# Evacuating PV results with four masked VectorE operations and one row-sum product, in a decode kernel bound by its loads

## Chip, cores, metric

One core of one Trainium2 chip. The metric is the device time of one execution in microseconds (us); medians of several runs. The kernel before had 366.29 us (three runs, 366.27 to 366.82).

## The reference

A gated mix of two branches for 8 sequences of one token, `D` = 576:

```python
a = attention(x, k_cache, v_cache, wq, wo)   # 32 query heads on 16 KV heads, head size 128,
                                             # last 2048 positions of each cache
b = mlp(layernorm(x), w1, b1, w2, b2)        # 576 -> 4608 -> 576, gelu
out = g * a + (1 - g) * b                    # g = sigmoid(sum(x * gate_w))
```

The K and V windows are 67 MB each, the weights 20 MB; each byte is used once.

## The kernel before

Operations are handed to a list scheduler, which fixes each engine's order when the program is built. At run time an engine takes its list in order: what stands behind an operation that waits doesn't run before it. Loads stream in one queue: `wq, w1`, 16 K tiles of 4 MB with 32 V units of 2 MB between them, `wo`, the last V units, then the four W2 chunks. A unit is one KV head for four sequences. PV is the product of the softmax's probabilities P with V; its evacuation is the step that takes the result out of PSUM (`ps`), where TensorE writes, into SBUF. For a pair of units the tail of the attention looks so:

```python
# TensorE: PV of one unit; p.V leaves 4 diagonal blocks (r) that still have to be added over rows
for t in range(16):
    mm = e.matmul(ps[c:c + 32, bk, :], PT[...], slot(s)[:, 512 * t:512 * t + 512], ...)
...
# after the second unit of the pair: all 512 columns to SBUF by ScalarE
u_ev[item] = add("act", lambda e: e.activation(out=EV[:, item % 2, :], in_=ps[:, bk, :]..., func=ACTF.Copy), ...)
# four fp32 products, one for each diagonal block
for r in range(4):
    mm = e.matmul(ps[:, BK_S, ...], EV[:, item % 2, 128 * r:128 * r + 128], i2[:, r, :, :]..., start=(r == 0), stop=(r == 3))
# then: small copy (ScalarE), product with 1/sum (GpSimd; VectorE for the last pair), and
def place(ch, bs, deps):      # sixteen tiny VectorE copies that put the heads where the projection wants them
    return [add("dve", ... e.tensor_copy(oT[32*q:32*q+32, ch, j, bs], oN[32*j:32*j+32, q, ch, bs]) ...)
            for j in range(4) for q in range(4)]

def project():                # four output projections; the c-th waits for the c-th set of copies
    for c in range(4):
        ...
        AccGroup("proj%d" % c, mms, place_done[c] + ds, cost=1.1)
# W2 products, as each chunk lands, accumulate in the same bank; then the final sum on VectorE
o_m2.append(AccGroup("m2_%d_%d" % (ci, n), mms, [o_hT, d], ...).op)
```

Of the kernel before, what the change touches and what calls it, by code (L numbers as in the profile page):

```python
# [7 lines left out]
F32 = mybir.dt.float32  # L8
ACTF = mybir.ActivationFunctionType
ALU = mybir.AluOpType  # L10
AXL = mybir.AxisListType
# [27 lines left out]
class _Plan:  # L39
# [10 lines left out]
    def add(self, eng, fn, deps=(), name=None, cost=0.1, after=(), prio=0):  # L50
        op = _Op(eng, fn, deps, name, cost, after=after, prio=prio)
        op.idx = len(self.all)
        self.all.append(op)
        return op
# [116 lines left out]
ARENA_BASE = 16512  # L171


def held_matmul(nc, e, out, lhsT, rhs, start=False, stop=True, skip=False, tile_size=(128, 128), tile_position=(0, 0)):
    return e.add_instruction(mybir.InstMatmult(
        name=nc.get_next_instruction_name(), engine=mybir.EngineType.PE,
        ins=[e.lower_ap(rhs), e.lower_ap(lhsT)], outs=[e.lower_ap(out)],
        start_tensor_calc=start, stop_tensor_calc=stop, is_transpose=False, bass_skip_group_check=skip,
        tile_size=tile_size, tile_position=tile_position, ldweights=False))


def build_kernel(nc, A_x, A_k_cache, A_v_cache, A_wq, A_wo, B_x, B_w1, B_b1, B_w2, B_b2, gate_w, out):
    B, Sq, D = A_x.shape
    _, Hkv, Sk, Dh = A_k_cache.shape
# [22 lines left out]
    with ExitStack() as es:  # L207
# [3 lines left out]
        def req(name, nelem, dt, align=64):  # L211
            sz = 2 if dt == BF else 4
            o = aoff[0] + ARENA_BASE
            o = (o + align - 1) // align * align - ARENA_BASE
            R[name] = (o, nelem, dt)
            aoff[0] = o + nelem * sz
# [17 lines left out]
        req("q4", 4 * 256, BF)  # L234
        req("qb", 2 * 8 * 4 * 32, BF)
        req("amask", 4, F32)
        req("b1T", FT, F32)
        req("b2", D, BF)
        req("hT", FT * 8, BF)
# [36 lines left out]
        def aoffs(name):  # L276
            return R[name][0] // 2
# [4 lines left out]
        def view(name, parts=128):  # L282
            o, n, dt = R[name]
            a = arena[0:parts, o // 2: o // 2 + (n * (2 if dt == BF else 4)) // 2]
            if dt == F32:
                a = a.bitcast(F32)
            return a
# [6 lines left out]
        i2 = view("i2").rearrange("p (r u m) -> p r u m", r=4, u=2)  # L294
# [6 lines left out]
        q4 = view("q4").rearrange("p (h m) -> p h m", h=4)  # L301
        qb = view("qb").rearrange("p (g n h m) -> p g n h m", g=2, n=8, h=4)
        amask = view("amask")
        b1T = view("b1T")
        b2_sb = view("b2", 8)
        u_sb, uh_sb, v1_sb, v2_sb = view("u"), view("uh"), view("v1"), view("v2")
# [15 lines left out]
        EV = view("EV").rearrange("p (u n) -> p u n", u=2)  # L322
# [7 lines left out]
        def slot(s):  # L330
            return RAW[:, s * SE:(s + 1) * SE]
# [12 lines left out]
        ps = es.enter_context(nc.psum_tensor("ps", [128, 8, 512], F32))  # L344
# [4 lines left out]
        BK_S = 6  # L349
        BK_ACC = 7  # L350
        OC = 64
# [6 lines left out]
        add, dma = P.add, P.dma  # L358
# [38 lines left out]
        for s in range(2):  # L397
            o_xz.append(add("dve", (lambda s=s: lambda e: e.tensor_copy(xz[:, s, :].rearrange("p (k z) -> p k z", z=2)[:, :, s], x_sb[:, 512:576]))(),  # L398
                            deps=dx + [o_xz0], name="xz%d" % s, cost=0.12))
# [12 lines left out]
        for s in range(2):  # L412
            o_yz.append(add("dve", (lambda s=s: lambda e: e.tensor_copy(yz[:, s, :].rearrange("p (k z) -> p k z", z=2)[:, :, s], y_bf[:, 512:576]))(),
                            deps=[o_y, o_yz0], name="yz%d" % s, cost=0.12))
# [30 lines left out]
        def b1ev_fn(e):  # L445
# [5 lines left out]
                   deps=[o_dga, o_dgb, o_onesf], name="g_pe", cost=0.4, after=[o_yTp])  # L451
# [7 lines left out]
        o_i20 = add("dve", lambda e: e.memset(view("i2"), 0.0), name="i2z", cost=0.1, prio=-1)  # L459
        o_i2 = [add("dve", (lambda q=q: lambda e: e.tensor_copy(i2[32 * q:32 * q + 32, :, q // 2, :], ident[32 * q:32 * q + 32, 32 * q:32 * q + 32].rearrange("p (r m) -> p r m", r=4)))(),  # L460
                    deps=[o_i20, o_ident], name="i2_%d" % q, cost=0.15, prio=-1) for q in range(4)]
        for q in range(4):
            o_i32.append(add("dve", (lambda q=q: lambda e: e.tensor_copy(i32[32 * q:32 * q + 32, :], ident[32 * q:32 * q + 32, 32 * q:32 * q + 32]))(),
                             deps=[o_ident, o_obl], name="i32_%d" % q, cost=0.15, prio=-1))
# [67 lines left out]
        o_hT = add("dve", hs_fn, deps=[o_hf, o_gb], name="hT", cost=0.4)  # L532
# [50 lines left out]
        u_ev, u_sum = {}, {}  # L583
        b6_w, b6_r = [], [o_yT, o_gb]
# [116 lines left out]
        def v_compute(i, s, d):  # L701
            g, q = divmod(i, 4)
            item = 2 * g + q // 2

            bk = BK_OS[item % 2]

            def pv_fn(e):
                mm = None
                for t in range(16):
                    c = 64 * (i % 2) + 32 * (t % 2)  # L710
                    mm = e.matmul(ps[c:c + 32, bk, :], PT[:, g % 2, 512 * q + 32 * t:512 * q + 32 * t + 32], slot(s)[:, 512 * t:512 * t + 512],  # L711
                                  start=(t < 2), stop=(t >= 14), skip_group_check=True, tile_position=(0, c))
                return mm
            deps = [d] + pt_done[g] + ([u_ev[item - 2]] if item >= 2 else o_qT + [o_u])
            prev = add("pe", pv_fn, deps=deps, name="pv%d" % i, cost=1.9, after=pv_hist[-1:])
            pv_hist.append(prev)
            slot_free[s] = [prev]
            if q == 3:
                pv_last[g] = prev
            if i % 2 == 0:  # L720
                return
            u_ev[item] = add("act", lambda e: e.activation(out=EV[:, item % 2, :], in_=ps[:, bk, :].rearrange("p (r d j) -> p r j d", r=4, j=4), func=ACTF.Copy),  # L722
                             deps=pv_hist[-2:] + ([u_sum[item - 2]] if item >= 2 else [o_hT]), name="uev%d" % item, cost=1.2, prio=3)

            def us_fn(e):
                mm = None
                for r in range(4):
                    mm = e.matmul(ps[:, BK_S, OC + 16 * (item % 2):OC + 16 * (item % 2) + 16], EV[:, item % 2, 128 * r:128 * r + 128], i2[:, r, :, :].rearrange("p u m -> p (u m)"),  # L728
                                  start=(r == 0), stop=(r == 3), skip_group_check=True)
                return mm  # L730
            u_sum[item] = add("pe", us_fn, deps=[u_ev[item]] + o_i2 + b6_r[-2:], after=b6_w[-1:], name="us%d" % item, cost=1.9, prio=3)
            b6_w.append(u_sum[item])
            if q % 2 == 1:
                hl = q // 2
                prev = u_sum[item]
                osrc = ps[:, BK_S, OC + 16 * (item % 2):OC + 16 * (item % 2) + 16]
                if item < Hkv - 1:
                    ev = add("act", lambda e: e.activation(out=o32[:, item % 2, :], in_=osrc, func=ACTF.Copy), deps=[prev] + ([oT_done[2 * item - 4], oT_done[2 * item - 3]] if item >= 2 else []), name="oev%d" % item, cost=0.25, prio=3)  # L738
                    o_item_ev[item] = ev
                    b6_r.append(ev)  # L740
                    eng, src_, deps = "pool", o32[:, item % 2, :], [ev, rg_done[g]]
                else:
                    eng, src_, deps = "dve", osrc, [prev, rg_done[g]]
                for t in (i - 1, i):
                    G, n = divmod(t, 8)

                    def om_fn(e, t=t, G=G, n=n):
                        dst = bass.AP(arena, offset=aoffs("oN") + 128 * (n % 2) + 8 * (n // 2) + 2 * G, ap=[[AST, 128], [1, 2], [32, 2], [64, 2]])
                        return e.tensor_tensor(out=dst, in0=src_[:, 8 * (t % 2):8 * (t % 2) + 8].rearrange("p (b l h) -> p b l h", b=2, l=2),  # L749
                                               in1=rg[:, g % 2, 8 * (t % 4):8 * (t % 4) + 8].rearrange("p (b l h) -> p b l h", b=2, l=2), op=ALU.mult)  # L750
                    oT_done[t] = add(eng, om_fn, deps=deps, name="oT%d" % t, cost=0.25, prio=9)
                if i == NUQ - 9:
                    place(slice(0, 8), slice(0, 6), list(oT_done.values()))
                elif i >= NUQ - 8:
                    c = (i % 8) // 2
                    place_done[c] = place(slice(c, 8, 4), slice(6, 8), [oT_done[i - 1], oT_done[i]])
# [3 lines left out]
        def place(ch, bs, deps):  # L760
            return [add("dve", (lambda j=j, q=q: lambda e: e.tensor_copy(oT[32 * q:32 * q + 32, ch, j, bs], oN[32 * j:32 * j + 32, q, ch, bs]))(), deps=deps, name="pl%d%d" % (j, q), cost=0.1, prio=2)  # L761
                    for j in range(4) for q in range(4)]
# [47 lines left out]
        pv_hist = []  # L810
# [81 lines left out]
```

## Time and profile before

| | before |
|---|---|
| time, median of 3 | 366.29 us |
| span in the profile | 364.9 us |
| read from HBM | 154.3 MB |
| last load landed (trace's landing records) | 362.58 us |
| final sum starts | 362.95 us |

The busy shares, the DMA row and the long chain are in the prediction. The tail of TensorE in the kernel before: start, length, engine, line, what it writes and reads, count, and in brackets the idle time ahead of it with what ended it. L711 is PV (16 products a unit), L728 the row sum, L555 the projections and the W2 products.

```profile
338.01 0.66 PE L555 MATMUL ps<-arena 128*8 128x288 bf16 x16 [0.23 <-DVE arena L761]
340.25 1.90 PE L711 MATMUL ps<-arena 128*32 128x512 bf16 x16 [1.58 <-DMA arena<-in_A_v_cache_dram]
...
350.07 1.90 PE L711 MATMUL ps<-arena 128*32 128x512 bf16 x16 [1.11 <-DMA arena<-in_A_v_cache_dram]
...
356.27 1.76 PE L555 MATMUL ps<-arena 128*8 128x288 bf16 x34 [1.35 <-DMA arena<-in_B_w_dram]
359.39 1.64 PE L555 MATMUL ps<-arena 128*8 128x288 bf16 x24 [1.35 <-DMA arena<-in_B_w_dram]
361.52 0.53 PE L555 MATMUL ps<-arena 128*8 128x288 bf16 x6 [0.49 <-DMA arena<-in_B_w_dram]
362.26 0.65 PE L555 MATMUL ps<-arena 128*8 128x288 bf16 x6 [0.20 <-DMA arena<-in_B_w_dram]
```

Every stretch at the end is released by a load ("DMA"): TensorE waits for the stream and not the other way round, and the last product ends 0.3 us after the last landing.

### The profile page before, as it was taken

The page shows a single profiled execution, that of the slowest core. Times are in us where ns is not written, and L with a number is a line of the kernel's source. Part 1 is how long each engine was busy: PE and PEld are TensorE (multiplying, and loading weights), DVE is VectorE, ACT ScalarE, POOL GpSimd, SP SyncE. Part 2 cuts the span into 40 slices and gives each one's busy share as a digit, 9 for nine tenths or more (in the row PEclk, how much of TensorE's full clock was granted, in tenths as well). Part 3 has the DMA queues.
Part 4 walks back from the last instruction along what each step waited for, and adds up shares of the span by engine and source line. Part 5 has one row for each costly group of instructions (what it writes and reads, how often), then busy time and mean ns, then how long its engine had stood idle before and what let it go on. Part 6 is the DMA issues. An engine that isn't in the chain of part 4 may idle for free.

```text
span 364.9 us, 3980 instructions
## 1 busy us (share of the span) xinstructions
PE 239.4 (66%) x1679; PEld 115.0 (32%) x1679; DVE 226.5 (62%) x340; ACT 22.4 (6%) x53; POOL 17.4 (5%) x80
## 2 busy tenths in 40 slices
PE   0269684838498938274959484738959297577575
PEld 0159331312143414022423232214424133234232
DVE  4700995675999280759965362789781739777221
ACT  1010000000000000000100000001100000001000
POOL 5021000001000000010000000000000000000000
PEclk9999998778589969596996978676978796859899
DMA  9999999999999999999999999999999999999995
GB/s 376 435 404 451 406 451 411 451 432 415 445 426 443 420 436 431 424 438 424 436 426 440 422 442 420 439 422 438 424 436 444 426 410 436 425 431 429 431 425 222
DMA packets 9690, 154.58 MB, mean 424 GB/s; under 512 B 1052, under 2 KB 1220, under 8 KB 2888
## 3 DMA queue, kind: packets, MB, share of 16 engines
q1 hardware_dynamic: 9616, 154.29, 98.9%
q8 instruction: 13, 0.21, 0.2%
q10 hardware_dynamic: 56, 0.03, 0.0%
q14 instruction: 5, 0.04, 0.0%
HBM read 154.31 MB, written 0.01 MB: 423 GB/s over the span
## 4 chain that ended last, share of the span: by engine, by line
DMA 62%; DVE 24%; PE 11%; issue 1%; SPq 0%; DVEq 0%
DMA arena<-in_A_k_cache_dram 54%; DVE arena L666 18%; PE ps L678 6%; DMA arena<-in_A_v_cache_dram 5%; PE ps L711 4%; DMA arena<-in_B_w_dram 4%; DVE arena L639 3%; DVE arena L597 1%; DVE arena L631 1%; DVE arena L600 0%; DVE arena L606 0%; PE ps L612 0%; DVE arena L614 0%; PE ps L555 0%; SPq L798 0%
## 5 line engine op out<-in xcount | busy, mean ns | idle before, releaser
L666 DVE STREAM_TRANSPOSE arena<-arena 128x4096 f32<-128x4096 f32 x32 | 140.7, 4424 | 85.4 <-DMA arena<-in_A_k_cache_dram 85.0
L678 PE MATMUL ps<-arena 128*32 128x512 bf16 x512 | 141.7, 440 | 62.7 <-DVE arena L666 62.7
L678 PEld LDWEIGHTS ps<-arena 128*32 128x32 bf16 x512 | 52.3, 105 | 144.7 <-DVE arena L666 67.7
L711 PE MATMUL ps<-arena 128*32 128x512 bf16 x512 | 60.7, 453 | 23.8 <-DVE arena L602 18.6
L711 PEld LDWEIGHTS ps<-arena 128*32 128x32 bf16 x512 | 24.8, 110 | 50.4 <-issue 31.7
L639 DVE STREAM_TRANSPOSE arena<-arena 128x512 bf16<-128x512 bf16 x32 | 30.8, 1019 | 0.0
L728 PE MATMUL ps<-arena 128*128 128x16 f32 x128 | 17.0, 264 | 5.6 <-ACT arena L722 3.9
L761 DVE COPY arena<-arena 32x4 bf16<-32x4 bf16 (+1 forms) x80 | 12.9, 161 | 10.1 <-POOL arena L749 7.9
L728 PEld LDWEIGHTS ps<-arena 128*128 128x128 f32 x128 | 15.5, 191 | 11.5 <-ACT arena L722 9.6
L722 ACT ACTIVATE arena<-ps 128x512 f32<-128x512 f32 x16 | 9.6, 598 | 148.9 <-PE ps L711 148.9
L749 POOL TENSOR_TENSOR arena<-arena 128x8 bf16<-128x8 f32 x30 | 5.9, 231 | 229.9 <-ACT arena L738 229.9
L597 DVE TENSOR_REDUCE arena<-ps 128x1 f32<-128x512 f32 x8 | 5.5, 692 | 12.2 <-PE ps L678 12.1
L510 PE MATMUL ps<-arena 128*128 128x8 bf16 x144 | 10.9, 201 | 2.6 <-DMA arena<-in_B_w_dram 2.6
L608 ACT ACTIVATE arena<-ps,arena 128x512 bf16<-128x512 f32 x8 | 5.5, 687 | 107.4 <-DVE arena L606 107.4
L510 PEld LDWEIGHTS ps<-arena 128*128 128x128 bf16 x144 | 10.8, 157 | 3.1 <-DMA arena<-in_B_w_dram 3.1
L555 PE MATMUL ps<-arena 128*8 128x288 bf16 (+1 forms) x140 | 9.3, 288 | 3.6 <-DMA arena<-in_B_w_dram 3.4
L659 POOL TENSOR_TENSOR arena<-arena 128x32 bf16<-128x32 bf16 x32 | 6.5, 240 | 86.0 <-PE ps L678 76.9
L612 PE MATMUL ps<-arena 128*128 128x32 f32 x16 | 3.9, 328 | 8.6 <-DVE arena L611 8.6
L631 DVE TENSOR_SCALAR arena<-arena 128x512 bf16<-128x512 bf16 x32 | 9.0, 324 | 0.0
L425 PE MATMUL ps<-arena 8*128 8x8 bf16 x8 | 0.6, 170 | 11.0 <-DVE arena L398 7.0
L512 PE MATMUL ps<-arena 128*128 128x8 bf16 x36 | 7.2, 201 | 0.0
L555 PEld LDWEIGHTS ps<-arena 128*8 128x8 bf16 (+1 forms) x140 | 4.6, 85 | 7.8 <-DMA arena<-in_B_w_dram 4.9
(84 smaller groups left out, 77.8 us busy)
## 6 DMA issues: line engine op xcount, KB each, us to landing
arena<-in_A_k_cache_dram SPq DMA_DIRECT2D x16, 4096.0 KB, 25.2
arena<-in_A_v_cache_dram SPq DMA_DIRECT2D x32, 2048.0 KB, 24.3
arena<-in_B_w_dram SPq DMA_DIRECT2D x1, 4608.0 KB, 24.1
arena<-in_A_wo_dram SPq DMA_DIRECT2D x4, 1152.0 KB, 10.0
arena<-in_A_wq_dram SPq DMA_DIRECT2D x1, 4096.0 KB, 13.4
arena<-in_B_w_dram SPq DMA_DIRECT2D x3, 1296.0 KB, 18.9
arena<-in_B_w_dram SPq DMA_DIRECT2D x2, 432.0 KB, 12.2
arena<-in_B_w_dram SPq DMA_DIRECT2D x1, 576.0 KB, 25.2
```

Of the source, the lines that this page charges most:

```text
L510: ins = e.matmul(out_, lhsT, yT[:, kt, :], start=(kt == 0), stop=False)
L512: ins = e.matmul(out_, lhsT, yT[:, 4 + c // 2, :], start=False, stop=True)
L555: ins = e.matmul(ps[c:c + 8, BK_ACC, 0:JN], lhsT, rhs[:, JN * j:JN * j + JN], start=False, stop=True, skip_group_check=True, tile_position ...
L597: mx = add("dve", lambda e: e.tensor_reduce(out=k(MX), in_=ps[:, bank, :], axis=AXL.X, op=ALU.max), deps=[qk_done[g]], name="mx%d" % g, co ...
L631: return e.tensor_scalar(out=dst, in0=view("Pd").rearrange("p (s n) -> p s n", s=2), scalar1=amask[:, a:a + 1], scalar2=None, op0=ALU.mult)
L639: return e.transpose(dst, src)
L666: tr = add("dve", (lambda h=h, kb=kb: lambda e: e.transpose(bass.AP(arena_f, offset=foffs("KT") + kb * SE // 2, ap=[[AST // 2, 128], [4, 1 ...
L678: mm = e.matmul(ps[32 * c:32 * c + 32, 2 * (G % 2) + nb, :], qb[:, G % 2, n, 2 * h + ee, :], rhs, start=(h == 0 and t == 0), stop=(h == 1 ...
L711: mm = e.matmul(ps[c:c + 32, bk, :], PT[:, g % 2, 512 * q + 32 * t:512 * q + 32 * t + 32], slot(s)[:, 512 * t:512 * t + 512], start=(t < 2 ...
L722: u_ev[item] = add("act", lambda e: e.activation(out=EV[:, item % 2, :], in_=ps[:, bk, :].rearrange("p (r d j) -> p r j d", r=4, j=4), fun ...
L728: mm = e.matmul(ps[:, BK_S, OC + 16 * (item % 2):OC + 16 * (item % 2) + 16], EV[:, item % 2, 128 * r:128 * r + 128], i2[:, r, :, :].rearra ...
L761: return [add("dve", (lambda j=j, q=q: lambda e: e.tensor_copy(oT[32 * q:32 * q + 32, ch, j, bs], oN[32 * j:32 * j + 32, q, ch, bs]))(), d ...
```

## The change

The intent: the row sum needs only the diagonal blocks. If VectorE multiplies each of the four column blocks by a 0/1 mask per row and adds them while it reads PSUM, 128 columns remain, and one fp32 product does what four did; ScalarE's 512-column copy goes.

```diff
-            u_ev[item] = add("act", lambda e: e.activation(out=EV[:, item % 2, :], in_=ps[:, bk, :].rearrange(...), func=ACTF.Copy),
-                             deps=..., name="uev%d" % item, cost=1.2, prio=3)
+            for r in range(4):
+                def ue_fn(e, r=r):
+                    dst = EV[:, item % 2, 0:128].rearrange("p (j d) -> p j d", j=4)
+                    src = ps[:, bk, 128 * r:128 * r + 128].rearrange("p (d j) -> p j d", j=4)
+                    if r == 0:
+                        return e.tensor_scalar(out=dst, in0=src, scalar1=rmask[:, 0:1], scalar2=None, op0=ALU.mult)
+                    return e.scalar_tensor_tensor(out=dst, in0=src, scalar=rmask[:, r:r + 1], in1=dst, op0=ALU.mult, op1=ALU.add)
+                u_ev[item] = add("dve", ue_fn, deps=deps, name="uev%d_%d" % (item, r), cost=0.25, prio=6)
+                deps = [u_ev[item]]
 ...
-                for r in range(4):
-                    mm = e.matmul(..., EV[:, item % 2, 128 * r:128 * r + 128], i2[:, r, :, :]..., start=(r == 0), stop=(r == 3))
-                return mm
+                return e.matmul(..., EV[:, item % 2, 0:128], usel, start=True, stop=True)
```

Cut: two small masks made at the start, and an unused function removed. The scheduler's costs change with it, and so does the order of other instructions, as the prediction tells.

## The prediction

> **What bounds the kernel now.** I read the strip of busy tenths first, then the DMA queue rows, then the chain that ended last, then the times from issue to landing of the two big loads, and last the waits of VectorE, the engine that the change loads.
>
> ```profile
> span 364.9 us, 3980 instructions
> PE 239.4 (66%) x1679; PEld 115.0 (32%) x1679; DVE 226.5 (62%) x340; ACT 22.4 (6%) x53; POOL 17.4 (5%) x80
> DMA  9999999999999999999999999999999999999995
> DMA packets 9690, 154.58 MB, mean 424 GB/s; under 512 B 1052, under 2 KB 1220, under 8 KB 2888
> q1 hardware_dynamic: 9616, 154.29, 98.9%
> DMA 62%; DVE 24%; PE 11%; issue 1%; SPq 0%; DVEq 0%
> ```
>
> The DMA row is 9 in every slice but the last, and one queue's packets take 98.9% of the 16 engines' span. No compute engine passes 66%. The kernel reads 154.3 MB once, and the span is about the time of that reading: successive 2 MB V loads land 4.84 us apart almost throughout (2.097 MB / 4.84 us = 433 GB/s), 4 MB K loads 9.67 us apart. What is not reading is small: about 2 us before the stream is up, and 2.3 us from the last landing (362.6) to the end.
>
> The chain gives VectorE 24%, but that does not make VectorE the bound. The chain can walk back through the instruction that allowed a load to be issued, and the load may then stand in the queue:
>
> ```profile
> 121.06 27.13 DMA arena<-in_A_k_cache_dram
> 196.19 29.87 DMA arena<-in_A_k_cache_dram
> 328.69 16.48 DMA arena<-in_A_v_cache_dram
> ```
>
> A 4 MB load needs 9.7 us by itself; the one issued at 121.06 landed 27.13 us later, so it stood 17.4 us behind earlier loads. Only that standing time is what a later issue can eat. Its smallest value is in the views of the two load lines (K first, V second):
>
> ```profile
> DMA to landing us min/median/max: 15.0/25.2/34.3
> DMA to landing us min/median/max: 13.6/24.3/34.4
> ```
>
> K: 15.0 - 9.7 = 5.3 us (the third K load, during startup). V: 13.6 - 4.8 = 8.7 us. Going through the issues in order with the landing time of the load ahead, the thin places are: third K load 5.3, seventh K load (issued 112.41) 6.7, first Wo pair 5.7, second Wo pair 6.4, V loads after 100 us 8.7, the last W2 chunk 10.8; the 11th and 15th K loads have 12.6 and 12.9. The queue is never empty.
>
> [...]
>
> **The change, part by part.** These rows carry it:
>
> ```profile
> L728 PE MATMUL ps<-arena 128*128 128x16 f32 x128 | 17.0, 264 | 5.6 <-ACT arena L722 3.9
> L722 ACT ACTIVATE arena<-ps 128x512 f32<-128x512 f32 x16 | 9.6, 598 | 148.9 <-PE ps L711 148.9
> L527 DVE SCALAR_TENSOR_TENSOR arena<-arena 128x288 f32<-128x288 f32 x1 | 0.5, 458 | 0.5 <-ACT arena L526 0.5
> ```
>
> Removed from ScalarE: 16 evacuations, 9.6 us; it is 6% busy, so nothing. Removed from TensorE: 64 fp32 products (two rows each, x128) become 16, so 128 rows become 32 and 17.0 us become about 17.0/4 = 4.3. It is idle a third of the time waiting for loads or transposes: nothing directly.
> Added to VectorE: 16 times one masked product (TENSOR_SCALAR) and three SCALAR_TENSOR_TENSOR on 128 columns. [...] Each waits for the one before; the chain shows 0.03 us between dependent VectorE instructions. [...] Two small reductions at the start (about 0.3 us each, as the similar 128x4 one at 286 ns) lie in VectorE's 4.1 us wait for the first inputs. Busy VectorE: 226.5 + 16 x 1.13 + 0.6 = 245, 67%.
>
> From end of PV to end of the row sum the path hardly changes: before 0.60 + 0.05 + 1.07 = 1.72 us (342.19 to 343.91); after 1.25 + 0.04 + about 0.4 for two fp32 rows (as the softmax sum, 0.41) = 1.7.
>
> What matters is where the static order of VectorE puts the evacuations, since each waits for its PV products and holds up all behind it. I compared the two orders. Most evacuations stand after a transpose pair and before a K tile that has not landed, inside this idle time:
>
> ```profile
> DVE arena L666 <- DMA arena<-in_A_k_cache_dram: 85.0, 11, 13.4
> ```
>
> The thin place is after the first softmax. K tiles are numbered from 0, so K6 is the seventh load. Before, K4's second transpose ran 108.0 to 112.4 and released the seventh K load at 112.41. After, the order is: first half of K4 to 102.3; evacuation 0 to 103.6; three softmax pieces to 104.3; evacuation 1, which needs the fourth PV unit, now placed directly behind the first three on TensorE: those end at 103.2, plus 1.8 gives 105.0, so evacuation to 106.2; the rest of the mask work, 0.8, to 107.0; four transposes of P, 3.9, to 110.9; then K4's second half, 4.4, to 115.3. The seventh K load is issued 2.9 us later; 6.7 - 2.9 = 3.8 us of queue remain[...]. No gap. The next evacuation waits for V5 (lands 114.3), and pushes K5's transposes about 5 us, to 126.1; K7's load has 17.4 us in hand, and VectorE is free again before K6 lands at 128.8.
> The same place in the rounds at 175 and 253 us has 12.6 and 12.9 us against a shift of about 3. Near 300 us an evacuation and sixteen small copies now stand ahead of K15's transposes: they end at about 300.3 against K15's landing at 299.9, so the second Wo pair loses some 0.4 of its 6.4. In the tail, PV of unit 31 ends at 352.0; evacuation to 353.3, row sum 353.7, product and copies 3.3, to 357.1: the same 357.1 as now (354.06 + 3.03), long before this:
>
> ```profile
> 362.95 0.45 DVE L826 TENSOR_TENSOR arena<-ps,arena 40x288 bf16<-40x288 f32 x1 [5.86 <-PE ps L555]
> ```
>
> The last W2 piece lands at 362.6 in both. Sum on the path that sets the end: 0 us, with perhaps 0.1 of noise in landings.
>
> **The rivals.**
> *VectorE starves the stream.* For: 20 us more on the engine that releases K slots, waits standing in front of transposes, and a margin at the seventh K load that halves. If one evacuation took 2 us and not 1.25, the shift there would be 2.9 + 1.5 and 2.3 us of queue would remain; at 3 us each the queue would run dry by some 2 us, once, and the time would be about 368. Against: one thin place only, the others hold three times the shift. Over 2% (7.3 us) would need about 13 us of shift there, or starvation in each round.
> *It gets faster.* For: TensorE loses 12.7 us, ScalarE 9.6, fp32 products fall to a quarter and the granted clock (0.841) may rise, so PV frees V slots sooner. Against: an earlier issue only stands longer in a full queue. Even with the ideal stream, 154.58 MB/433 GB/s = 357.0 us, the whole reserve is 8 us, mostly startup and end, which the change does not touch. It would make 365.9 at best.
> *The tail moves.* For: evacuation 14 stands behind 32 copies, each set 3.0 us, and the last projection is now behind the first W2 group. Against: 5.9 us of idle before the final sum. It would have to lose all of that; then 367.
>
> **Range and chances.** The stream decides: 366.29 before, so 366.3. Three runs before spread over 0.55 us. Downward there is little; upward a dry moment at the seventh K load or a late tail could give 1 us. Range 365.7 to 367.3. Faster by over 2%: 0.01; slower by over 2%: 0.03; same: 0.96.
>
> **What would show it.** Right: DMA row still 9 throughout and about 99%; VectorE busy near 245 us, TensorE near 227, ScalarE near 13;[...] row-sum products x32 near 4.3 us; the smallest K issue-to-landing now that of the seventh K load, about 13.5 (16.35 before, less 2.9); VectorE's wait for K smaller by 10 to 20 us. Wrong: a DMA slice below 9 near 117 to 120 us, K loads landing over 10 us apart there, a K load whose issue-to-landing falls to 10 to 11 us, a VectorE wait of several us on PV products, or the wait before the final sum falling to zero.

The sum came to 1.13 us for the four operations of an evacuation, 1.25 us with the waits between them, 20 us for sixteen; "1.13", "1.25" and all that is worked out with them are the author's estimate. What the trace shows of the stream is V loads landing 4.84 us apart and a queue that is not empty; that nothing on the engines could speed it was thus argued, not shown.

## The result

370.48 us median (369.30 to 371.32, four runs) against 366.49 (366.27 to 366.82, four runs). The ratio is 1.0106, 95% interval 1.0076 to 1.0136. Ratios here are the mean time of one kernel's runs over that of the other's of the same rounds, so not quite the ratio of the medians. The time is 4 us longer and outside the range; it is within 2%, as forecast.

The page of the changed kernel:

```profile
span 368.9 us, 3837 instructions
PE 231.8 (63%) x1583; PEld 104.3 (28%) x1583; DVE 248.6 (67%) x406; ACT 12.8 (3%) x37; POOL 17.5 (5%) x80
DMA  9999999999999999999999999999999999999992
DMA 39%; DVE 37%; PE 20%; issue 2%; SPq 0%; POOL 0%; ACT 0%; DVEq 0%
L726 DVE TENSOR_SCALAR arena<-ps,arena 128x128 f32<-128x128 f32 x16 | 5.4, 337 | 26.8 <-PE ps L709 26.8
L727 DVE SCALAR_TENSOR_TENSOR arena<-ps,arena 128x128 f32<-128x128 f32 x48 | 16.8, 351 | 1.7
L732 PE MATMUL ps<-arena 128*128 128x16 f32 x32 | 6.3, 273 | 10.0 <-DVE arena L727 7.2
```

The DMA row is as full as before except for its last digit, 2 and not 5: the loads end in time and then something else runs on. The trace's landing records say the same: last landing 363.05 us, 0.47 later than before; end of the span 368.9, 4.0 later. So 3.5 of the 4 us lie behind the last landing. The masked operations take 337 and 351 ns. The mean granted clock is 0.852, where it was 0.841.

Now the same part of TensorE's timeline as above, in the changed kernel (L709 is PV, L732 the row sum, L553 projections and W2):

```profile
341.23 0.90 PE L553 MATMUL ps<-arena 128*8 128x288 bf16 x16 [2.40 <-DVE arena L763]
341.92 3.39 PE L709 MATMUL ps<-arena 128*32 128x512 bf16 x16
346.91 0.40 PE L732 MATMUL ps<-arena 128*128 128x16 f32 x2 [1.61 <-DVE arena L727]
...
351.11 0.66 PE L553 MATMUL ps<-arena 128*8 128x288 bf16 x16 [1.97 <-DVE arena L763]
351.61 3.47 PE L709 MATMUL ps<-arena 128*32 128x512 bf16 x16
...
357.01 1.27 PE L553 MATMUL ps<-arena 128*8 128x288 bf16 x18
360.50 6.35 PE L553 MATMUL ps<-arena 128*8 128x288 bf16 x70 [2.22 <-DVE arena L763]
```

From 341 us on nothing is released by a load any more. The last line is the loss: the fourth projection waits for the sixteen copies (L763), and 54 W2 products, whose weights had landed from 356.7 on, stand behind it in TensorE's list. Before, they ran as they landed. And the whole block runs slowly: 70 products take 6.35 us. The next view shows why. Its columns are the window, its length, busy time (instructions) of TensorE, its weight loads, VectorE, ScalarE and GpSimd, then the granted TensorE clock, DMA share and GB/s. First the kernel before, then the changed one:

```profile
358.00:363.00 5.00, 2.86 (x38) 1.31 (x36) 0.05 (x1) 0.41 (x1) 0.00 (x0) 1.00 0.59 229
```

```profile
341.50:344.90 3.40, 3.40 (x30) 1.34 (x20) 0.00 (x0) 0.00 (x0) 0.00 (x0) 0.50 1.00 429
351.80:355.20 3.40, 3.40 (x20) 1.03 (x16) 0.08 (x1) 0.00 (x0) 0.00 (x0) 0.50 1.01 429
358.60:362.00 3.40, 1.50 (x22) 0.88 (x24) 1.57 (x10) 0.31 (x1) 0.00 (x0) 0.50 0.81 321
362.00:365.40 3.40, 3.40 (x32) 1.90 (x30) 0.00 (x0) 0.10 (x1) 0.00 (x0) 0.50 0.05 19
```

Half clock, in pieces of 3.4 us, exactly where the PV units (3.39 and 3.47 us, 1.90 before) and the last block run.

The bill of the tail, from the two timelines. First VectorE's last copies, before and changed, and the final sum of the changed kernel:

```profile
354.06 3.03 DVE L761 COPY arena<-arena 32x4 bf16<-32x4 bf16 x16
```

```profile
357.42 3.03 DVE L763 COPY arena<-arena 32x4 bf16<-32x4 bf16 x16
366.89 0.45 DVE L828 TENSOR_TENSOR arena<-ps,arena 40x288 bf16<-40x288 f32 x1 [6.44 <-PE ps L553]
```

The final sum starts 366.89 - 362.95 = 3.94 us later. Before, the last sixteen copies end at 354.06 + 3.03 = 357.09; in the changed kernel at 360.45, 3.36 later. From there to the final sum is 6.44 us now and 5.86 before, 0.58 more. Of the 3.36, PV unit 31 ends 3.11 later (355.08 against 351.97): it starts 1.54 later, since the third projection, waiting for its copies until 351.11, stands ahead of it, and V31 lands 0.49 later; and it takes 1.57 longer at half clock. The rest, 0.25, is the longer evacuation less the shorter row sum.

The middle of the kernel went nearly as worked out. VectorE's largest waits in the changed kernel:

```profile
DVE arena L664 <- DMA arena<-in_A_k_cache_dram: 45.6, 10, 13.7
DVE arena L726 <- PE ps L709: 26.8, 7, 7.6
```

The first was 85.0 us before: waiting for K tiles has in part become waiting for PV, without a price. The seventh K load was issued at 115.19 (predicted 115.3), and there the stream did run dry: that load landed 10.8 us behind the one ahead of it, not 9.7.

### The profile page after: what moved, and what is told of

Read it like the earlier page. It is cut to its first block, busy times and chain, and to the rows that moved or that the text cites. A ratio compares the mean times of both kernels' runs of the same rounds, so it can differ in the third digit from the quotient of the medians. Undisturbed runs are those within 1.5% of the kernel's fastest.

```text
span 368.9 us, 3837 instructions
## 1 busy us (share of the span) xinstructions
PE 231.8 (63%) x1583; PEld 104.3 (28%) x1583; DVE 248.6 (67%) x406; ACT 12.8 (3%) x37; POOL 17.5 (5%) x80
## 4 chain that ended last, share of the span: by engine, by line
DMA 39%; DVE 37%; PE 20%; issue 2%; SPq 0%; POOL 0%; ACT 0%; DVEq 0%
DMA arena<-in_A_k_cache_dram 29%; DVE arena L664 17%; PE ps L676 12%; DMA arena<-in_A_v_cache_dram 10%; DVE arena L637 7%; PE ps L709 6%; DVE arena L763 3%; DVE arena L727 2%; PE ps L553 2%; DVE arena L595 2%; DVE arena L629 1%; DVE arena L598 1%; DVE arena L604 1%; DVE arena L726 1%; DVE arena L612 1%
## 5 line engine op out<-in xcount | busy, mean ns | idle before, releaser
L676 PE MATMUL ps<-arena 128*32 128x512 bf16 x512 | 135.6, 426 | 48.4 <-DVE arena L664 48.4
L709 PE MATMUL ps<-arena 128*32 128x512 bf16 x512 | 64.4, 467 | 40.9 <-DVE arena L600 18.9
L676 PEld LDWEIGHTS ps<-arena 128*32 128x32 bf16 x512 | 50.2, 102 | 127.4 <-DVE arena L664 55.2
L709 PEld LDWEIGHTS ps<-arena 128*32 128x32 bf16 x512 | 25.2, 113 | 71.9 <-issue 41.8
L726 DVE TENSOR_SCALAR arena<-ps,arena 128x128 f32<-128x128 f32 x16 | 5.4, 337 | 26.8 <-PE ps L709 26.8
L727 DVE SCALAR_TENSOR_TENSOR arena<-ps,arena 128x128 f32<-128x128 f32 x48 | 16.8, 351 | 1.7
L763 DVE COPY arena<-arena 32x4 bf16<-32x4 bf16 (+1 forms) x80 | 12.9, 162 | 6.0 <-POOL arena L751 3.8
L553 PE MATMUL ps<-arena 128*8 128x288 bf16 (+1 forms) x140 | 10.2, 350 | 6.9 <-DVE arena L763 6.9
L508 PE MATMUL ps<-arena 128*128 128x8 bf16 x144 | 10.9, 201 | 3.0 <-DMA arena<-in_B_w_dram 3.0
L732 PE MATMUL ps<-arena 128*128 128x16 f32 x32 | 6.3, 273 | 10.0 <-DVE arena L727 7.2
L508 PEld LDWEIGHTS ps<-arena 128*128 128x128 bf16 x144 | 10.8, 158 | 3.5 <-DMA arena<-in_B_w_dram 3.5
L732 PEld LDWEIGHTS ps<-arena 128*128 128x128 f32 x32 | 4.8, 188 | 16.4 <-DVE arena L727 10.6
L553 PEld LDWEIGHTS ps<-arena 128*8 128x8 bf16 (+1 forms) x140 | 5.3, 99 | 12.2 <-DVE arena L763 8.5
L740 ACT ACTIVATE arena<-ps 128x16 f32<-128x16 f32 x15 | 2.8, 184 | 165.8 <-PE ps L732 164.8
```

The costliest lines, as they stand in the source:

```text
L508: ins = e.matmul(out_, lhsT, yT[:, kt, :], start=(kt == 0), stop=False)
L553: ins = e.matmul(ps[c:c + 8, BK_ACC, 0:JN], lhsT, rhs[:, JN * j:JN * j + JN], start=False, stop=True, skip_group_check=True, tile_position ...
L676: mm = e.matmul(ps[32 * c:32 * c + 32, 2 * (G % 2) + nb, :], qb[:, G % 2, n, 2 * h + ee, :], rhs, start=(h == 0 and t == 0), stop=(h == 1 ...
L709: mm = e.matmul(ps[c:c + 32, bk, :], PT[:, g % 2, 512 * q + 32 * t:512 * q + 32 * t + 32], slot(s)[:, 512 * t:512 * t + 512], start=(t < 2 ...
L726: return e.tensor_scalar(out=dst, in0=src, scalar1=rmask[:, 0:1], scalar2=None, op0=ALU.mult)
L727: return e.scalar_tensor_tensor(out=dst, in0=src, scalar=rmask[:, r:r + 1], in1=dst, op0=ALU.mult, op1=ALU.add)
```

## The experiments

**Theories.** *Tail*: the 4 us come from the last four evacuations, which make the copies late, with the projections ahead of PV units and W2 products in TensorE's list, and the half clock that follows on idle. *Stream* (the first rival): 20 us more on VectorE starve the loads, which the gap at the seventh K load shows, and the tail only inherits it. A third came up later: fewer fp32 products leave TensorE less active, and that alone drops the clock.

Kernels ran beside runs of the kernel before: 366.08 median for the first four, 366.26 for the next four, 366.21 for the next three, 366.22 for the last. The changed kernel is compared with the others through the kernel before. All results are correct. "Behind" is the move of an operation in an engine's list, after the scheduler; `("pe", "proj3", "m2_2_0")` puts `proj3` behind `m2_2_0` on TensorE. `proj0` to `proj3` are the four projections, `pv29` is PV of unit 29, `us1` the row sum of pair 1, `m2_2_0` the W2 group of the third chunk, `tr4_1` the second transpose of tile K4:

```diff
+        for eng, name, behind in self.moves:      # in schedule(), ahead of the semaphore counts
+            seq = self.order[eng]
+            op = next(o for o in seq if o.name == name)
+            seq.remove(op)
+            seq.insert(next(n for n, o in enumerate(seq) if o.name == behind) + 1, op)
 ...
```

| run | median us | lowest to highest | ratio to before (95%) | last landing | final sum |
|---|---|---|---|---|---|
| before | 366.49 | 366.27 to 366.82 | | 362.58 | 362.95 |
| changed | 370.48 | 369.30 to 371.32 | 1.0106 (1.0076, 1.0136) | 363.05 | 366.89 |
| x1_proj3_late | 366.79 | 366.44 to 368.90 | 1.0029 (0.9999, 1.0058) | 364.09 | 365.60 |
| x2_tail_old | 366.25 | 366.15 to 367.43 | 1.0013 (0.9995, 1.0031) | 362.54 | 362.92 |
| x3_tail_new | 369.22 | 367.27 to 370.09 | 1.0076 (1.0045, 1.0107) | 362.55 | 364.04 |
| x4_k6 | 370.57 | 369.90 to 371.24 | 1.0120 (1.0100, 1.0140) | 362.66 | 366.28 |
| x5_warm | 366.73 | 366.52 to 368.43 | 1.0021 (0.9998, 1.0044) | 362.38 | 362.76 |
| x6_projs_late | 366.70 | 366.10 to 367.05 | 1.0013 (0.9997, 1.0030) | 362.42 | 362.80 |
| x7_best | 366.79 | 366.09 to 368.24 | 1.0018 (0.9994, 1.0041) | 362.81 | 363.18 |
| x8_more_dve | 371.32 | 370.16 to 371.60 | 1.0130 (1.0113, 1.0147) | 366.54 | 366.92 |
| x9_four_products | 372.33 | 371.10 to 372.84 | 1.0160 (1.0131, 1.0188) | 362.85 | 368.28 |
| x10_proj01_late | 368.07 | 367.38 to 368.80 | 1.0048 (1.0025, 1.0071) | 364.09 | 365.49 |
| x11_old_12_13 | 368.19 | 366.67 to 368.84 | 1.0045 (1.0014, 1.0075) | 363.07 | 364.21 |
| x12_before_proj3 | 366.74 | 366.23 to 368.56 | 1.0027 (0.9996, 1.0057) | 362.55 | 363.48 |

The last two columns are from each profiled execution alone; between executions of one kernel the last landing moves by up to about 1 us.

**x1_proj3_late.** Changed kernel, `("pe", "proj3", "m2_2_0")`: one move.

> The changed kernel with one move in TensorE's order: the last output projection (which waits for the last sixteen copies on VectorE, done at 360.5 in the changed kernel's trace) now stands behind the third W2 group and not behind the first. Tail theory (the 4 us are W2 products held up in TensorE's queue behind that projection): the last W2 product ends near 363.5 instead of 366.9, VectorE's final sum starts there, time 366.8 to 367.6, so 3 us under the changed kernel. Stream theory (the loads lost the time in the middle, VectorE too busy): no change, 370.0 to 370.8.

366.79: 3.7 us gone with one move in one list. The W2 products do hold the end when they stand behind the copies. The profiled execution happened to be the slowest of the four (368.90), with the clock at 0.50 from 358 to 363; the other three lie at 366.44 to 367.04.

**x2_tail_old.** Changed kernel with `if item >= 12:` the old evacuation and four products.

> The changed kernel, but the last four evacuations (pairs 12 to 15) as before: one ScalarE copy and four fp32 products; the other twelve stay new. Tail theory: 366.6 to 367.3, the final sum about 2.3 us before the end and within 1 us of the last landing. Stream theory: 369.5 to 370.8, since all the evacuations that stand among the K transposes are kept.

366.25, a little under the expected range and the same as before within 0.2%. Twelve evacuations among the K transposes cost nothing that can be measured. The stream theory falls here. The scheduler also put the fourth projection back behind the second W2 group in this run, and ahead of it in x3, so these two runs do not tell evacuations from place; x1, x6 and x12 do.

**x3_tail_new.** The kernel before with only `item >= 12` new.

> The kernel before, but with only the last four evacuations new. Tail theory: it has most of the loss, 369.2 to 370.3, with the last landing at 362.5 as in the kernel before. Stream theory: 366.3 to 367.0.

369.22, the counterpart: most of the loss without any change in the middle, last landing as before. The runs spread (367.27 to 370.09); the profiled one is the fastest, and in it PV unit 31 ran at full clock (1.90 us).

**x4_k6.** Changed kernel, `("dve", "uev1_*", "tr4_1"), ("pe", "us1", "pv5")`.

> The changed kernel with the second evacuation moved behind the second transpose of tile K4 on VectorE (and its row sum behind the sixth PV unit on TensorE), so that the seventh K load is issued near 113.5 and not 115.2. Tail theory with a small gap in the stream: the 1.1 us by which that load lands late goes, the last landing comes 0.5 to 1 us earlier, and so does the end: 369.3 to 370.2. Stream theory: this gap is the start of the loss, 366.5 to 368.

The gap went: the seventh K load was issued at 113.53, landed 9.67 us behind its forerunner, and the last landing came 0.4 us earlier. The time did not, against my expectation: 370.57. A gap, where there is one, is hidden by the tail in the changed kernel.

**x5_warm.** Changed kernel, its order kept, plus products that nobody uses:

```diff
+        def warm_fn(e):
+            for _ in range(10):
+                mm = e.matmul(ps[:, 0, 0:320], ident, ones_bf, start=True, stop=True, ...)
+            return mm       # five of these: ahead of proj1, us14, proj2, us15 and proj3
```

> The changed kernel with its order kept, plus five idle-fillers of ten 320-column products each on TensorE, in the places of the tail where it waits for VectorE. They compute nothing that is used. Clock theory (half of the tail's loss is the granted clock, which falls to 0.5 after idle stretches and makes the last 70 products take 6.35 us): the clock stays at 1.0 there, the last 70 products take 3.5 to 4.2 us and the units of PV 1.9 us, time 366.5 to 368.3. Order theory alone (only the place of the projections counts): 369.5 to 371, since the order is the same.

366.73. TensorE in that kernel (L716 PV, L836 the fillers, L560 projections and W2), and a window of it as above:

```profile
351.28 1.89 PE L716 MATMUL ps<-arena 128*32 128x512 bf16 x16
...
356.30 1.53 PE L836 MATMUL ps<-arena 128*128 128x320 bf16 x10
358.58 4.13 PE L560 MATMUL ps<-arena 128*8 128x288 bf16 x70 [0.75 <-DVE arena L770]
```

```profile
358.60:362.00 3.40, 3.40 (x64) 2.44 (x64) 0.00 (x0) 0.41 (x1) 0.00 (x0) 1.00 0.67 259
```

Same order, same 70 products behind the copies: but the clock stays at 1.00, PV unit 31 takes 1.89 us, the copies end at 358.5, and the 70 products take 4.13 us and end with the last landing. The idle stretches of the changed kernel were no longer than 2.4 us each; filling them with 1.5 us of work each was enough. One of four runs had 368.43, so the cure is not certain in every execution.

**x6_projs_late.** Changed kernel, `("pe", "proj0", "pv29"), ("pe", "proj1", "proj0"), ("pe", "proj2", "pv31"), ("pe", "proj3", "m2_2_0")`.

> The changed kernel with all four projections moved back on TensorE so that none stands ahead of a PV unit: the first two behind PV unit 29, the third behind unit 31, the fourth behind the third W2 group. Tail theory: the end is again set by the last landing, final sum within 3.5 us of it, 366.3 to 367.2, and not above the run where only the fourth was moved (366.79). If the evacuations themselves and not the products behind the copies cost the time: 368.5 to 370.5.

366.70, with the narrowest spread of the mended orders. The end in the profile is that of the kernel before: final sum 0.4 us behind the last landing. All sixteen new evacuations are in it, so these do not cost the time as such.

**x7_best.** x6 and x4 together.

> Both moves together: all projections late, and the second evacuation behind K4's second transpose. No gap at the seventh K load, end set by the last landing: 366.0 to 366.8, equal to the kernel before within 0.2%. It cannot be below it by more than 0.2%, since the stream is as full as before.

366.79: no better than x6. I expected up to 0.3 us from closing the gap; the landings of this execution do not show it (362.81 against 362.42), so it is below what varies anyway. In fact x6 had nothing to close: its seventh K load was issued at 113.91 and landed 9.67 us behind its forerunner. No version beats the kernel before.

**x8_more_dve.** x2 with six more masked products in each of the twelve evacuations:

```diff
-                for r in range(4):
+                for n, r in enumerate((0, -1, -2, -3, -1, -2, -3, 1, 2, 3)):   # r < 0: into unused columns of EV
 ...
```

Cut: the place that each writes to, and two moves on VectorE that put the second transposes of tiles K10 and K14 right behind the first.

> The kernel with the last four evacuations as before, and six more masked products (results unused) in each of the twelve new evacuations: about 2.3 us more in each, 27 us more on VectorE, same order. It asks how much more VectorE work the stream can bear. If the margin at the seventh K load is what counts (5.2 us ahead of the queue's end in that kernel, less two times 2.3, and a gap opens below some 4.5): the seventh K load lands 3 to 4.5 us late and the time is 369.3 to 371.3. If VectorE has slack enough: 366.2 to 367.

371.32, a true loss in the stream, for comparison with the changed kernel's. Its page and its chain:

```profile
DMA  9999999999998999999999999999999999999995
GB/s 400 430 422 407 430 453 419 432 426 425 458 412 340 402 409 446 407 457 410 448 416 432 416 455 416 446 414 446 424 430 432 434 408 435 407 433 426 438 419 205
```

The thirteenth slice drops to 8 and 340 GB/s, and the last digit is 5 again. The seventh K load was issued 0.61 us ahead of its forerunner's landing and landed 2.5 us late by the last of its landing records, 3.3 by the first; the whole stream ends 4.0 us later than in x2 (the rest was lost at loads with 10 us and more in hand, so not by a late issue), and the final sum comes 0.4 us after it. This is what the first rival would have looked like.

**x9_four_products.** Changed kernel, the one row-sum product issued four times over.

> The changed kernel, but each row sum is computed four times over by the same fp32 product (same result), so TensorE has as many fp32 products as before. It asks whether taking the products away let the granted clock fall in the tail. If their activity matters: the clock in the last 7 us is back at 1.0 in most runs, 366.5 to 368.5. If only the order of the copies and the projections matters: 0.66 us more per pair on the tail's chain, no better than the changed kernel, 370 to 372.

372.33, just above the range. The clock was halved under the last block as before (70 products took 6.34 us), and the chain is 0.66 us longer for each pair. The third theory falls: giving the products back, 0.66 us of work a pair, does not keep the clock up in this order.

**x10_proj01_late.** Changed kernel, `("pe", "proj0", "pv29"), ("pe", "proj1", "proj0")` alone.

> The changed kernel with only the first two projections moved, behind PV unit 29; the third and fourth stay where they were. Tail theory, chain part: PV unit 29 no longer waits for the 32 copies, the copies ahead of the fourth projection end at 357 to 358.5 and not 360.5, fewer W2 products are held up, 366.6 to 368.3. If the loss is made only at the fourth projection's place: 369.5 to 370.8.

368.07: 2.4 us of the 4. PV unit 29 runs when V29 has landed, but in the profiled execution unit 31 took 3.59 us at half clock, the copies ended at 359.2, and the 70 products took 6.23 us.

**x11_old_12_13.** Changed kernel with `if item in (12, 13):` the old evacuation.

> The changed kernel with pairs 12 and 13 evacuated as before and 14 and 15 new, order otherwise as in the changed kernel (fourth projection ahead of the second W2 group). If the late 32 copies behind evacuations 12 and 13 start the delay: they end near 338 and not 341, PV unit 29 runs when V29 has landed, time 366.3 to 368.3. If the last two evacuations make it: 369 to 370.8.

368.19: 2.3 us of the 4. The first 32 copies were back at 338.6, yet units 29 and 30 ran at half clock (3.04 and 3.60 us), and the 70 products still took 5.59 us. The expected times of x10 and x11 held (x10's copies ended later than the 357 to 358.5 expected), and neither end of the tail explains the loss alone.

**x12_before_proj3.** The kernel before, `("pe", "proj3", "m2_0_0")`: the fourth projection where the changed kernel has it.

> The kernel before with one move: the fourth projection stands ahead of the second W2 group, as in the changed kernel. Its copies end at 357.1 there, 3.4 us earlier than in the changed kernel. If the place alone is what costs: 369 to 371. If the place costs only because the copies come late: the W2 products catch up while loads still land, 366.0 to 367.0; a run in which the clock is halved there may reach 368.

366.74. Here too 70 products stand behind the copies and run at half clock:

```profile
356.89 6.55 PE L562 MATMUL ps<-arena 128*8 128x288 bf16 x70 [2.22 <-DVE arena L768]
```

But they start at 356.9, 3.6 us earlier than in the changed kernel, and when they end 6.55 us later, the last load has landed only 0.9 us before: 0.5 us is lost. So the place of the projection is dear only with late copies.

## Why the prediction was wrong

**Right.** The bound: the stream. V loads land about 4.85 us apart almost throughout in the changed kernel, as before, and no gain came from 9.6 us less on ScalarE and 7.6 less on TensorE. The middle: the seventh K load at 115.19 (115.3 worked out), K5's transposes done at 126.36 (126.1), VectorE 248.6 us busy (245), TensorE 231.8 (227). The 115.19 is in part luck: the two evacuations held VectorE 0.35 us longer together than worked out, and the wait of 0.7 us for the fourth PV unit did not occur; eight profiles with this order on VectorE (the changed kernel, x1, x2, x5, x6, x9, x10, x11) have the issue between 113.90 and 115.21. That the twelve evacuations among the transposes are free is shown by x2. No starvation cost measurable time in the changed kernel: shown by x4. Of the signs, the wait for K fell by 39.4 us and not by 10 to 20, VectorE's longest wait for PV was 7.6 us, the seventh K load took 14.64 us to land and not 13.5, and the copies near 300 us ended at 301.7 and not 300.3; none of this set the end. The sign named for the tail, a wait before the final sum that falls to zero, did not come: it rose to 6.44.

**The step that failed.** "In the tail, PV of unit 31 ends at 352.0; evacuation to 353.3, row sum 353.7, product and copies 3.3, to 357.1 [...] long before this", and with it "Sum on the path that sets the end: 0 us". The copies ended at 360.45. Three things were left out.
First, I took the end of unit 31 over from the old trace. I had the new order at hand, in which unit 29 stands behind the second projection, which waits for 32 copies behind evacuation 13, and unit 31 behind the third; I did not run it through. (The first three projections stood ahead of units 29 and 31 before, too; new is that their copies come later.) x10 and x11, each undoing one half of that, recover 2.4 and 2.3 us.
Second, I let PV take 1.9 us. At half clock it took 3.4 to 3.6 (3.39 and 3.47 in the changed kernel, 3.59 in x10, 3.60 in x11), and the clock halved after pieces with long waits in them: ahead of the three falls of the tail TensorE was busy for 0.93, 1.43 and 1.75 us of 3.4 (a piece with 1.79 had no fall behind it). In x5 it was busy for 2.48 us or more in each piece from 338.1 to 362, and the clock stayed at 1.00. x5 shows that this is not a side matter: with the clock held up, the bad order costs nothing that can be measured (1.0021, 0.9998 to 1.0044).
Third, I read VectorE's 5.86 us wait ahead of the final sum as slack ("It would have to lose all of that"). It is a wait for TensorE, and behind the fourth projection TensorE has 70 products to do: 4.13 us at full clock (x5), 6.35 mostly at half (changed kernel). To end with the last landing at about 362.5, the copies may end at 362.5 - 4.1 = 358.4 or at 362.5 - 6.4 = 356.1. They ended at 357.1 before: the slack was 1.3 us in one case and none in the other. Moving the fourth projection (x1) gives the slack back.
I had named the place, in the third rival, and priced it by the wrong idle time.

**A smaller term, mis-sized.** "3.8 us of queue remain [...] No gap." What it took for enough was not shown. The lead was 3.88 us, as worked out, and a gap opened. A load leaves 16 landing records; by the first of them this one was 0.8 us late, by the last 1.1. The lead in several runs, issue to landing of the load ahead, against the lateness by the first record: 4.84 none, 4.75 0.1, 4.28 0.3, 3.99 0.6, 3.88 0.8, 0.61 3.3. By this measure it opens near 4.7 us in these runs; by the last record 4.28 is still only 0.1 late and 3.99 is 1.0. The landing that I measured against is the last of 16 records which, for the load ahead, are spread over 1.7 us, so part of the lead was not there. It cost 0.4 us of the last landing at most (x4, one profile of each), and no measured time. In the first rival, "at 3 us each the queue would run dry by some 2 us" does not follow from its own numbers: 6.7 - 2.9 - 3.5 leaves 0.3 us of queue.

**Others.** An evacuation takes 1.51 us (345.35 to 346.86), not 1.25: 337 and 351 ns an operation, 1.39 us for the four, where my estimate was 1.13. The row sums take 6.3 us and not 4.3: two rows alone take 0.40 us (eight took 1.07). 128 columns took VectorE 337 ns, ScalarE's copy of 512 took 598: 2.63 against 1.17 ns a column.

**Left open.** How the clock's 3.4 us pieces fall differs between executions; this is probably why x1, x3, x5 and x12 have single runs 2 us off, but only one execution of each was profiled, so it is argued and not shown.

## What to carry to other kernels

The slack of a tail is not the idle time of the engine that ends it: run the in-order list of the engine that it waits for, with the new times, and count all that stands behind the late instruction. When a change makes TensorE wait longer near the end, price the work that follows at half clock too (here 6.35 us, mostly at half, against 4.13). And where the stream is the bound, keep instructions that wait for a long chain (here a projection waiting for copies) behind those that wait only for a load.
